# A's key weights by whole rows in one tile, with ScalarE's second weight load held back by a one-column copy

## The chip, the cores and the metric

The kernel runs on one core of one Trainium2 chip. The metric is device time in microseconds (us), the median over several executions. The hardware profiler records every instruction with its start and every DMA packet. The profiled span (470.8 us before) is about 2 us shorter than the device time of the same execution (472.58 us); the two are not mixed below.

The change can move well under 1 us of 473. A device time does not settle that: unaltered executions of the kernel before in one set of rounds ran from 472.62 to 473.16 us. So most of this study reads one mark in the profile: **the start of the 256th and last key matmul**. TensorE works without a pause from there to the end.

## The reference, cut to what matters

```python
def reference(A_x, A_wqkv, A_wo, B_x, B_wqkv, B_wo, gate_w):
    x = A_x                                    # 1 x 2048 x 1024, bf16
    g = sigmoid((x * gate_w).sum(-1))          # one gate per token
    a = linear_attention_A(x, A_wqkv, A_wo)    # 32 heads; phi(k) = where(k > 0, k + 1, exp(k)) + 1e-6
    b = sliding_attention_B(x, B_wqkv, B_wo)   # window 8, dilation 2
    return g * a + (1 - g) * b
```

The change touches only the first stage of A: the keys, `x @ A_wqkv[:, 1024:2048]`, then phi. In TensorE's terms, 16 token tiles (t) times 2 column halves times 8 contraction rows (kt, 128 each) give 256 matmuls of 128x512.

## The kernel before

The first loads. SyncE (`nc.sync`) and ScalarE (`nc.scalar`) each issue DMAs; `dma_start_transpose` delivers x with the contraction dimension on the partitions.

```python
    WkA = [wpool.tile([P, KT, 512], BF16, name=f"WkA{h}", tag="wa") for h in range(2)]

    def load_xT(k, t0, t1):        # two contraction rows, tokens of tiles t0..t1
        nc.sync.dma_start_transpose(out=xT[:, 2 * k:2 * k + 2, t0 * P:t1 * P],
                                    in_=rows(x, t0 * P, t1 * P)[:, 2 * k * P:(2 * k + 2) * P])

    def load_wk(eng, k, h):        # two contraction rows of one column half: 256 KB in runs of 1 KB
        eng.dma_start(out=WkA[h][:, 2 * k:2 * k + 2, :], in_=A_wqkv[..., D + 512 * h:D + 512 * h + 512] ...)

    with tc.manual_schedule(engines={SP, mybir.EngineType.Activation}):
        load_wk(nc.scalar, 0, 0)
        first_act = consts.tile([P, 1], BF16, name="first_act")
        nc.scalar.activation(out=first_act[:], in_=ones[:, 0:1], func=ACT.Exp)
        load_wk(nc.scalar, 0, 1)
        load_xT(0, 0, 2)
        load_xT(0, 2, 4)
        for k in range(1, 4):
            load_wk(nc.sync, k, 0)
            load_xT(k, 0, 4)
            load_wk(nc.sync, k, 1)
        ...                        # x for the other twelve token tiles, x by rows, later weights
```

The first matmuls, on eight PSUM banks, so that four token tiles and both halves advance together as the rows arrive:

```python
            warm_up(37)            # 37 matmuls of 128x128 on a constant
            first = [bank_k(i) for i in range(8)]
            for k in range(4):
                for half in range(2):
                    for t in range(4):
                        for kt in (2 * k, 2 * k + 1):
                            project(first[4 * half + t], t, kt, half)
                        if k == 3:
                            phi(work, pk[:, t, half * 512:(half + 1) * 512], first[4 * half + t])
            ...                    # token tiles 4 to 15, eight matmuls per bank
```

The softmax here doesn't subtract the row's maximum and nothing guards it: scores larger than these inputs give would overflow.

Of the kernel before, what the change touches and what calls it, by code (L numbers as in the profile page):

```python
# [8 lines left out]
ACT = mybir.ActivationFunctionType  # L9
ALU = mybir.AluOpType  # L10
BF16 = mybir.dt.bfloat16
# [4 lines left out]
P = 128  # L16
# [23 lines left out]
def kernel(  # L40
# [11 lines left out]
    nc = tc.nc  # L52
    S, D = A_x.shape[1:]
    assert D == 1024 and S == 2048

    x = A_x[0].rearrange("(m two) d -> two m d", two=2)
    out2 = out[0].rearrange("(m two) d -> two m d", two=2)

    def rows(ap, s0, s1):
        return ap[s0 // 1024, s0 % 1024:(s1 - 1) % 1024 + 1, :]  # L60
# [3 lines left out]
    KT = D // P  # L64
# [4 lines left out]

    consts = ctx.enter_context(tc.tile_pool(name="consts", bufs=1))  # L70
    wpool = ctx.enter_context(tc.tile_pool(name="wpool", bufs=2))
    dram = ctx.enter_context(tc.tile_pool(name="dram", bufs=1, space=bass.MemoryType.DRAM))
    big = ctx.enter_context(tc.tile_pool(name="big", bufs=1))
    ps_pj = ctx.enter_context(tc.tile_pool(name="ps_pj", bufs=4, space=bass.MemoryType.PSUM))

    def load_w(name, src, col0, tag, only=(0, 1)):
        halves = []
        for h in only:
            w = wpool.tile([P, KT, 512], BF16, name=f"{name}{h}", tag=tag)
            c0 = col0 + h * 512  # L80
            nc.sync.dma_start(out=w[:], in_=src[:, c0:c0 + 512].rearrange("(kt p) n -> p kt n", p=P))  # L81
            halves.append(w)
        return halves

    xT = big.tile([P, KT, S], BF16, name="xT", tag="xT")
    xrow = big.tile([P, NB, D], BF16, name="xrow", tag="vV")

    def load_rows(eng, t0, t1):
        eng.dma_start(out=xrow[:, t0:t1, :], in_=rows(x, t0 * P, t1 * P).rearrange("(t p) d -> p t d", p=P))  # L89

    WkA = [wpool.tile([P, KT, 512], BF16, name=f"WkA{h}", tag="wa") for h in range(2)]

    def load_xT(k, t0, t1):
        nc.sync.dma_start_transpose(out=xT[:, 2 * k:2 * k + 2, t0 * P:t1 * P],  # L94
                                    in_=rows(x, t0 * P, t1 * P)[:, 2 * k * P:(2 * k + 2) * P])

    def load_wk(eng, k, h):
        eng.dma_start(out=WkA[h][:, 2 * k:2 * k + 2, :],  # L98
                      in_=A_wqkv[2 * k * P:(2 * k + 2) * P, D + 512 * h:D + 512 * h + 512]
                      .rearrange("(kt p) n -> p kt n", p=P))  # L100

    ones = nc.const_aps.tensor(1.0, [P, P], BF16)
    with tc.manual_schedule(engines={SP, mybir.EngineType.Activation}):
        load_wk(nc.scalar, 0, 0)
        first_act = consts.tile([P, 1], BF16, name="first_act")
        nc.scalar.activation(out=first_act[:], in_=ones[:, 0:1], func=ACT.Exp)
        load_wk(nc.scalar, 0, 1)
        load_xT(0, 0, 2)
        load_xT(0, 2, 4)
        for k in range(1, 4):  # L110
            load_wk(nc.sync, k, 0)
            load_xT(k, 0, 4)
            load_wk(nc.sync, k, 1)
        for t in range(4, NB):
            nc.sync.dma_start_transpose(out=xT[:, :, t * P:(t + 1) * P], in_=rows(x, t * P, (t + 1) * P))  # L115
        for t in range(0, NB, 4):
            load_rows(nc.sync, t, t + 4)
        gw_row = consts.tile([P, D], BF16, name="gw_row")
        nc.sync.dma_start(out=gw_row[:], in_=gate_w.partition_broadcast(P))  # L119
        WvA = load_w("WvA", A_wqkv, 2 * D, "wb")  # L120
        WoA = load_w("WoA", A_wo, 0, "wo")
        WvB = load_w("WvB", B_wqkv, 2 * D, "wc")
    WqA = load_w("WqA", A_wqkv, 0, "wa")



# [13 lines left out]
    for slot in range(2):  # L140
        nc.gpsimd.memset(qsel[:, slot:slot + 1], 0.0)
        for pair in range(2):
            r = 64 * pair + 32 * slot
# [9 lines left out]
    def phi(work, dst, pj):  # L153
        e = work.tile([P, 512], F32, name="e", tag="e")
        nc.scalar.activation(out=e[:], in_=pj[:], func=ACT.Exp)  # L155
        nc.vector.tensor_scalar(out=e[:], in0=e[:], scalar1=1.0, scalar2=1e-6, op0=ALU.min, op1=ALU.add)  # L156
        nc.vector.scalar_tensor_tensor(out=dst, in0=pj[:], scalar=0.0, in1=e[:], op0=ALU.max, op1=ALU.add)

    with tc.manual_schedule(engines={PE}):

        with ExitStack() as s1:
# [4 lines left out]
            s1.enter_context(tc.manual_schedule(engines={DVE}))  # L166
            pk = big.tile([P, NB, D], BF16, name="pk", tag="pkO")
            def project(pj, t, kt, half):
                nc.tensor.matmul(pj[:], lhsT=xT[:, kt, t * P:(t + 1) * P], rhs=WkA[half][:, kt, :],  # L169
                                 start=(kt == 0), stop=(kt == KT - 1))  # L170

            def warm_up(n):
# [7 lines left out]
            def bank_k(i):  # L180
                return (ps_1.tile([P, 512], F32, name="pk1_ps", tag="p1") if i & 4 else
                        ps_pj.tile([P, 512], F32, name="pk_ps", tag="pj"))

            first = [bank_k(i) for i in range(8)]
            for k in range(4):
                for half in range(2):
                    for t in range(4):
                        for kt in (2 * k, 2 * k + 1):
                            project(first[4 * half + t], t, kt, half)
                        if k == 3:  # L190
                            phi(work, pk[:, t, half * 512:(half + 1) * 512], first[4 * half + t])
            for t in range(4, NB):
                for half in range(2):
                    pj = bank_k(2 * t + half)
                    for kt in range(KT):
                        project(pj, t, kt, half)
                    phi(work, pk[:, t, half * 512:(half + 1) * 512], pj)
# [6 lines left out]
            for t in range(1, NB):  # L204
                side.append(lambda t=t: nc.vector.tensor_tensor(
                    out=zacc[:], in0=zacc[:] if t > 1 else pk[:, 0, :], in1=pk[:, t, :], op=ALU.add))
            side.append(lambda: nc.gpsimd.partition_all_reduce(zrow[:], zacc[:], P, bass_isa.ReduceOp.add))
            for t in range(NB):
                side.append(lambda t=t: nc.vector.tensor_tensor_reduce(
                    out=gjunk[:], in0=xrow[:, t, :], in1=gw_row[:], scale=1.0, scalar=0.0, op0=ALU.mult,  # L210
# [3 lines left out]
            for half in range(2):  # L214
                g_ = junk.tile([P, KT, 512], BF16, name=f"G{half}", tag=f"G{half}")
                G.append(g_)
                for kt in range(KT):
                    pj = ps_pj.tile([P, 512], F32, name="g_ps", tag="pj")
                    for t in range(NB):
                        nc.tensor.matmul(pj[:], lhsT=xrow[:, t, kt * P:(kt + 1) * P],  # L220
                                         rhs=pk[:, t, half * 512:(half + 1) * 512],
# [12 lines left out]
            for g in range(2):  # L234
                kvp = ps_pj.tile([P, 512], F32, name="kv_ps", tag="pj")[:, 0:256].rearrange("p (c d) -> p c d", c=4)
                for c in range(4):
                    for kt in range(KT):
                        for j in range(2):
                            cols = slice(c * P + 64 * j, c * P + 64 * j + 64)
                            nc.tensor.matmul(kvp[64 * j:64 * j + 64, c, :], lhsT=WvA[g][:, kt, cols],  # L240
                                             rhs=G[g][:, kt, cols], start=(kt == 0), stop=(kt == KT - 1))
# [84 lines left out]
            def qa_units(t, bank, evacuate):  # L326
                def mm(half, kt, st):
                    if kt == 0:
                        st["pj"] = bank()
                    nc.tensor.matmul(st["pj"][:], lhsT=xT[:, kt, t * P:(t + 1) * P], rhs=WqA[half][:, kt, :],  # L330
                                     start=(kt == 0), stop=(kt == KT - 1))
                    if kt == KT - 1:
                        evacuate(t, half, st["pj"])
                for half in range(2):
                    st = {}
                    for kt in range(KT):
                        yield lambda half=half, kt=kt, st=st: mm(half, kt, st)
# [24 lines left out]
        with ExitStack() as s2:  # L362
# [163 lines left out]
            for c in range(KT):  # L526
                kts[c] = kpool.tile([P, 2, 1024], BF16, name="kt", tag="kt")
                for hh in range(2):
# [3 lines left out]
                    if 1 <= c <= 2:  # L532
                        t = 2 * (c - 1) + hh
                        nc.sync.dma_start_transpose(out=pqT[0][:, :, t * P:(t + 1) * P],
                                                    in_=pqd[t * P:(t + 1) * P, :])
                    if 4 <= c < 7:
# [6 lines left out]
                              in_=B_wo[4 * P:, 512:1024].rearrange("(k p) n -> p k n", p=P))  # L543
            raw = wpool.tile([P, 4, D], BF16, name="raw", tag="wc")
            fw = wpool.tile([P, 2, D], F32, name="fw", tag="wc")
            lw = wpool.tile([P, 4, D], BF16, name="lw", tag="wa")

            def qa_output(t, half):
                def lhsT(r, kt, j):
                    return xT[64 * r:64 * r + 64, kt, t * P + 64 * j:t * P + 64 * j + 64]  # L550

                def rhs(r, kt):
                    return WqA[half][64 * r:64 * r + 64, kt, :]

                def evacuate(ps, part):
                    if part == 0:
                        nc.scalar.copy(out=raw[:, t - 12, half * 512:(half + 1) * 512], in_=ps[:])
                return lhsT, rhs, evacuate
# [5 lines left out]
        with ExitStack() as s3:  # L564
# [54 lines left out]
            for i, p_ in enumerate(parts):  # L619
# [4 lines left out]
                f = out_part(i, *p_)  # L624
# [33 lines left out]
```

## Time and profile before

| | before |
|---|---|
| device time, median of 6 | 472.86 us (472.62 to 473.16) |
| profiled span | 470.8 us |
| TensorE busy | 465.1 us (99%) |
| last warm-up matmul starts | 4.63 us |
| first x piece has landed | 5.43 us |
| first / last key matmul starts | 5.48 / 60.52 us |

A semaphore is the counter that a DMA raises as its parts arrive and that an engine waits for; "landed" is the last of the sixteen semaphore records of a DMA. Those records, and starts to the hundredth, are read from the trace itself.

The first lines of the page of the kernel before. Section 1 gives each engine's busy time; of section 2 two rows are shown, where each digit is the busy tenths of one of 40 slices.

```profile
## 1 busy us (share of the span) xinstructions
PE 465.1 (99%) x5735; PEld 249.2 (53%) x5765; DVE 277.2 (59%) x600; ACT 169.7 (36%) x274; POOL 15.3 (3%) x30
## 2 busy tenths in 40 slices
PE   8999999999999999999999999999999999999997
...
DMA  8999970000644243527327525432563913211001
```

TensorE has no room except in the first slice and at the very end. The first slice, as the timeline shows it: columns are start in us, length in us, engine, line, operation, count, and in brackets how long the engine had been idle and what ended that. SPq and ACTq are the DMA issues of SyncE and ScalarE.

```profile
0.80 2.61 SPq L94 DMA_TRANSPOSE xT<-in_A_x_dram  x2
...
0.82 0.97 ACTq L98 DMA_DIRECT2D WkA<-in_A_wqkv_dram  x2
0.83 4.11 PE L175 MATMUL warm<-const-bfloat16-1.0 128*128 128x128 bf16 x37 [0.83 <-PEq L642]
...
2.09 0.20 ACT L106 ACTIVATE first_act<-const-bfloat16-1.0 128x1 bf16<-128x1 bf16 x1
3.46 0.58 SPq L98 DMA_DIRECT2D WkA<-in_A_wqkv_dram  x1
4.09 1.24 SPq L94 DMA_TRANSPOSE xT<-in_A_x_dram  x1
...
5.47 7.73 PE L169 MATMUL pk_ps<-WkA,xT 128*128 128x512 bf16 x34 [0.53 <-DMA xT<-in_A_x_dram]
```

Two things are to be seen. The key matmuls wait 0.53 us for x (0.73 us after the array could have taken the next matmul, 4.74), and then never again. And both of ScalarE's loads are issued at once, from 0.82 to 1.79: the Activation written between them holds nothing back, because it runs at 2.09, when the second load is already gone. (The idle time in brackets counts from the end of the matmul before, which the profile models. The other waits in the text count from start to start, less the usual pace, and so come out about 0.2 us longer.)

The same stretch by microseconds, with the DMA rate in the last column (columns: stretch, its length, TensorE's busy time and matmuls, granted clock, mean busy share of the DMA engines, GB/s):

```profile
core 0: us, PE busy (x), PEclk, DMA share, GB/s
2.50:3.50 1.00, 1.00 (x12) 1.00 1.09 309
3.50:4.50 1.00, 1.00 (x12) 1.00 1.13 327
4.50:5.50 1.00, 0.47 (x6) 1.00 1.00 227
5.50:6.50 1.00, 1.00 (x5) 1.00 1.11 251
```

### The profile page before, as it was taken

The page shows a single profiled execution, that of the slowest core. Times are in us where ns is not written, and L with a number is a line of the kernel's source. Part 1 is how long each engine was busy: PE and PEld are TensorE (multiplying, and loading weights), DVE is VectorE, ACT ScalarE, POOL GpSimd, SP SyncE. Part 2 cuts the span into 40 slices and gives each one's busy share as a digit, 9 for nine tenths or more (in the row PEclk, how much of TensorE's full clock was granted, in tenths as well). Part 3 has the DMA queues.
Part 4 walks back from the last instruction along what each step waited for, and adds up shares of the span by engine and source line. Part 5 has one row for each costly group of instructions (what it writes and reads, how often), then busy time and mean ns, then how long its engine had stood idle before and what let it go on. Part 6 is the DMA issues. An engine that isn't in the chain of part 4 may idle for free.

```text
span 470.8 us, 13145 instructions
## 1 busy us (share of the span) xinstructions
PE 465.1 (99%) x5735; PEld 249.2 (53%) x5765; DVE 277.2 (59%) x600; ACT 169.7 (36%) x274; POOL 15.3 (3%) x30
## 2 busy tenths in 40 slices
PE   8999999999999999999999999999999999999997
PEld 5444444445444444444677677777764444444444
DVE  0586689990319999999567676767670049800000
ACT  1343321112533333334555555555551134221121
POOL 2300000500000000000000000000000000000000
PEclk9999999999999999999999999999999999999999
DMA  8999970000644243527327525432563913211001
GB/s 208 207 237 377 349 254 0 0 1 1 208 141 123 79 143 125 155 97 250 104 55 111 109 48 94 101 88 57 92 167 73 232 59 79 71 53 46 34 33 46
DMA packets 98732, 55.40 MB, mean 118 GB/s; under 512 B 70130, under 2 KB 90610, under 8 KB 98674
## 3 DMA queue, kind: packets, MB, share of 16 engines
q1 hardware_dynamic: 93378, 49.87, 40.6%
q10 hardware_dynamic: 5296, 4.69, 2.9%
q8 instruction: 45, 0.74, 0.7%
q14 instruction: 13, 0.11, 0.1%
HBM read 26.10 MB, written 15.86 MB: 89 GB/s over the span
## 4 chain that ended last, share of the span: by engine, by line
PE 85%; SPq 11%; DMA 2%; DVE 1%; issue 1%; ACT 0%; DVEq 0%
PE q_ps L389 27%; PE d_ps L593 12%; PE e_ps L593 11%; PE g_ps L220 11%; PE p_ps L294 11%; PE p_ps L330 8%; SPq L115 4%; SPq L81 4%; DMA WvB<-in_B_wqkv_dram 2%; PE po L468 2%; PE s2b L446 2%; SPq L94 1%; SPq L119 1%; SPq L98 1%; SPq L89 1%
## 5 line engine op out<-in xcount | busy, mean ns | idle before, releaser
L389 PE MATMUL q_ps<-xT,WqB 64*64 64x512 bf16 x1024 | 69.0, 377 | 0.0
L389 PE MATMUL q_ps<-xT,WkB 64*64 64x512 bf16 x1024 | 68.5, 376 | 0.0
L156 DVE TENSOR_SCALAR e<-e 128x512 f32<-128x512 f32 x64 | 27.1, 423 | 65.9 <-ACT e L155 65.9
L294 PE MATMUL p_ps<-WvB,xT 128*128 128x512 bf16 x250 | 57.3, 379 | 0.4
L169 PE MATMUL pk_ps<-WkA,xT 128*128 128x512 bf16 x251 | 55.2, 379 | 0.8 <-DMA xT<-in_A_x_dram 0.5
L220 PE MATMUL g_ps<-pk,xrow 128*128 128x512 bf16 x251 | 55.2, 379 | 0.3
L451 ACT ACTIVATE PT<-s2b 128x928 bf16<-128x928 f32 (+4 forms) x40 | 34.1, 854 | 45.2 <-PE s2b L446 45.2
L453 DVE TENSOR_TENSOR PT<-PT,mask 128x928 bf16<-128x928 bf16 (+4 forms) x40 | 23.6, 590 | 35.9 <-ACT PT L451 35.9
L330 PE MATMUL p_ps<-WqA,xT 128*128 128x512 bf16 x188 | 43.0, 379 | 0.2
L593 PEld LDWEIGHTS <-pqT 128*128 128x128 bf16 x272 | 26.0, 98 | 29.7 <-issue 0.4
L593 PEld LDWEIGHTS <-OBT 128*128 128x128 bf16 x272 | 26.0, 98 | 29.4
L169 PEld LDWEIGHTS <-xT 128*128 128x128 bf16 x256 | 25.0, 98 | 30.8 <-DMA xT<-in_A_x_dram 0.8
L220 PEld LDWEIGHTS <-xrow 128*128 128x128 bf16 x256 | 25.0, 98 | 30.2
L294 PEld LDWEIGHTS <-xT 128*128 128x128 bf16 x256 | 24.8, 98 | 30.2 <-issue 0.7
L389 PEld LDWEIGHTS <-WkB 64*64 64x64 bf16 x1024 | 32.6, 107 | 12.4 <-DMA vd<-tmp 0.2
L389 PEld LDWEIGHTS <-WqB 64*64 64x64 bf16 x1024 | 31.6, 107 | 11.1 <-issue 0.2
L600 DVE TENSOR_SCALAR osb<-e_ps,omg 128x128 bf16<-128x128 f32 x1 | 0.3, 350 | 57.6 <-PE e_ps L593 57.6
L155 ACT ACTIVATE e<-pk_ps 128x512 f32<-128x512 f32 x32 | 18.9, 597 | 40.4 <-PE pk_ps L169 36.1
L299 ACT CAST tmp<-p_ps 128x512 bf16<-128x512 f32 x32 | 18.7, 588 | 36.4 <-PE p_ps L294 32.5
L593 PE MATMUL d_ps<-WoA,pqT 128*128 128x512 bf16 (+1 forms) x133 | 30.7, 369 | 0.2
L593 PE MATMUL d_ps<-WoB,OBT 128*128 128x512 bf16 (+1 forms) x134 | 30.7, 369 | 0.1
L330 PEld LDWEIGHTS <-xT 128*128 128x128 bf16 x192 | 18.8, 98 | 22.7
(63 smaller groups left out, 528.5 us busy)
## 6 DMA issues: line engine op xcount, KB each, us to landing
vd<-tmp SPq DMA_DIRECT2D x16, 264.0 KB
xrow<-in_A_x_dram SPq DMA_DIRECT2D x4, 1024.0 KB
out_dram<-osb ACTq DMA_DIRECT2D x31, 128.0 KB
pqd<-tmp SPq DMA_DIRECT2D x12, 256.0 KB
WvA<-in_A_wqkv_dram SPq DMA_DIRECT2D x2, 1024.0 KB
WoA<-in_A_wo_dram SPq DMA_DIRECT2D x2, 1024.0 KB
WvB<-in_B_wqkv_dram SPq DMA_DIRECT2D x2, 1024.0 KB
WqA<-in_A_wqkv_dram SPq DMA_DIRECT2D x2, 1024.0 KB
```

Of the source, the lines that this page charges most:

```text
L81: nc.sync.dma_start(out=w[:], in_=src[:, c0:c0 + 512].rearrange("(kt p) n -> p kt n", p=P))
L115: nc.sync.dma_start_transpose(out=xT[:, :, t * P:(t + 1) * P], in_=rows(x, t * P, (t + 1) * P))
L155: nc.scalar.activation(out=e[:], in_=pj[:], func=ACT.Exp)
L156: nc.vector.tensor_scalar(out=e[:], in0=e[:], scalar1=1.0, scalar2=1e-6, op0=ALU.min, op1=ALU.add)
L169: nc.tensor.matmul(pj[:], lhsT=xT[:, kt, t * P:(t + 1) * P], rhs=WkA[half][:, kt, :], start=(kt == 0), stop=(kt == KT - 1))
L220: nc.tensor.matmul(pj[:], lhsT=xrow[:, t, kt * P:(kt + 1) * P], rhs=pk[:, t, half * 512:(half + 1) * 512], start=(t == 0), stop=(t == NB - 1))
L294: nc.tensor.matmul(st["pj"][:], lhsT=xT[:, kt, t * P:(t + 1) * P], rhs=WvB[half][:, kt, :], start=(kt == 0), stop=(kt == KT - 1))
L330: nc.tensor.matmul(st["pj"][:], lhsT=xT[:, kt, t * P:(t + 1) * P], rhs=WqA[half][:, kt, :], start=(kt == 0), stop=(kt == KT - 1))
L389: nc.tensor.matmul(banks[o][64 * j:64 * j + 64, :], lhsT=lhsT(r, kt, j), rhs=rhs(r, kt), start=first and kt == 0, stop=kt == KT - 1, skip_ ...
L451: nc.scalar.activation(out=pt[:, :, 0:W_], in_=s2b[:].rearrange("p a b s -> p (a b) s")[:, :, 0:W_], func=ACT.Exp, scale=SCALE)
L453: nc.vector.tensor_tensor(out=pt[:, :, 0:W_], in0=pt[:, :, 0:W_], in1=mask[:, None, base:base + W_].broadcast_to([P, 4, W_]), op=ALU.mult)
L593: nc.tensor.matmul(st["ps"][:, 0:n], lhsT=lhsT, rhs=W[c0 // 512][:, c, c0 % 512:c0 % 512 + n], start=(side == 0 and c == 0), stop=(side == ...
```

## The change

The intent: one tile of whole rows instead of two of column halves, so that each weight run is 2 KB and the first step needs just row 0 of the weights and row 0 of x; the second load of ScalarE (now row 2) is really held back, by a copy that writes one column of its destination, so that x row 0 does not share the queues with it; the rest of the weights is threaded between x pieces of one or two rows. The order of the first 64 matmuls follows. `WqA`, which reuses the space, becomes one tile too.

```diff
@@ -88,29 +89,29 @@
     def load_rows(eng, t0, t1):
         eng.dma_start(out=xrow[:, t0:t1, :], in_=rows(x, t0 * P, t1 * P).rearrange("(t p) d -> p t d", p=P))
 
-    WkA = [wpool.tile([P, KT, 512], BF16, name=f"WkA{h}", tag="wa") for h in range(2)]
-
-    def load_xT(k, t0, t1):
-        nc.sync.dma_start_transpose(out=xT[:, 2 * k:2 * k + 2, t0 * P:t1 * P],
-                                    in_=rows(x, t0 * P, t1 * P)[:, 2 * k * P:(2 * k + 2) * P])
-
-    def load_wk(eng, k, h):
-        eng.dma_start(out=WkA[h][:, 2 * k:2 * k + 2, :],
-                      in_=A_wqkv[2 * k * P:(2 * k + 2) * P, D + 512 * h:D + 512 * h + 512]
-                      .rearrange("(kt p) n -> p kt n", p=P))
+    WkA = wide.tile([P, KT, D], BF16, name="WkA", tag="wa")
+
+    def load_xT(kt, n, t0, t1):
+        nc.sync.dma_start_transpose(out=xT[:, kt:kt + n, t0 * P:t1 * P],
+                                    in_=rows(x, t0 * P, t1 * P)[:, kt * P:(kt + n) * P])
+
+    def load_wk(eng, kt):
+        eng.dma_start(out=WkA[:, kt, :], in_=A_wqkv[kt * P:(kt + 1) * P, D:2 * D])
 
     ones = nc.const_aps.tensor(1.0, [P, P], BF16)
     with tc.manual_schedule(engines={SP, mybir.EngineType.Activation}):
-        load_wk(nc.scalar, 0, 0)
-        first_act = consts.tile([P, 1], BF16, name="first_act")
-        nc.scalar.activation(out=first_act[:], in_=ones[:, 0:1], func=ACT.Exp)
-        load_wk(nc.scalar, 0, 1)
-        load_xT(0, 0, 2)
-        load_xT(0, 2, 4)
-        for k in range(1, 4):
-            load_wk(nc.sync, k, 0)
-            load_xT(k, 0, 4)
-            load_wk(nc.sync, k, 1)
+        load_wk(nc.scalar, 0)
+        nc.scalar.copy(out=WkA[:, 2, 0:1], in_=ones[:, 0:1])
+        load_wk(nc.scalar, 2)
+        load_xT(0, 1, 0, 4)
+        load_wk(nc.sync, 1)
+        load_xT(1, 1, 0, 4)
+        load_xT(2, 2, 0, 4)
+        load_wk(nc.sync, 3)
+        for kt in (4, 6):
+            load_wk(nc.sync, kt)
+            load_xT(kt, 2, 0, 4)
+            load_wk(nc.sync, kt + 1)
         for t in range(4, NB):
             nc.sync.dma_start_transpose(out=xT[:, :, t * P:(t + 1) * P], in_=rows(x, t * P, (t + 1) * P))
         for t in range(0, NB, 4):
@@ -120,7 +121,10 @@
         WvA = load_w("WvA", A_wqkv, 2 * D, "wb")
         WoA = load_w("WoA", A_wo, 0, "wo")
         WvB = load_w("WvB", B_wqkv, 2 * D, "wc")
-    WqA = load_w("WqA", A_wqkv, 0, "wa")
+    WqA = wide.tile([P, KT, D], BF16, name="WqA", tag="wa")
+    for h in range(2):
+        nc.sync.dma_start(out=WqA[:, 4 * h:4 * h + 4, :],
+                          in_=A_wqkv[512 * h:512 * h + 512, 0:D].rearrange("(kt p) n -> p kt n", p=P))
 
 
 
@@ -182,12 +186,12 @@
                         ps_pj.tile([P, 512], F32, name="pk_ps", tag="pj"))
 
             first = [bank_k(i) for i in range(8)]
-            for k in range(4):
+            for kts_ in ((0,), (1,), (2, 3), (4, 5), (6, 7)):
                 for half in range(2):
                     for t in range(4):
-                        for kt in (2 * k, 2 * k + 1):
+                        for kt in kts_:
                             project(first[4 * half + t], t, kt, half)
-                        if k == 3:
+                        if kts_[-1] == KT - 1:
                             phi(work, pk[:, t, half * 512:(half + 1) * 512], first[4 * half + t])
             for t in range(4, NB):
                 for half in range(2):
... (the same indexing change where WqA and the tile lw are used; a new pool for the wide tile)
```

More of the change, by code (lines that the diff above doesn't have):

```diff
@@ L71 @@
     wpool = ctx.enter_context(tc.tile_pool(name="wpool", bufs=2))
+    wide = ctx.enter_context(tc.tile_pool(name="wide", bufs=1))
     dram = ctx.enter_context(tc.tile_pool(name="dram", bufs=1, space=bass.MemoryType.DRAM))
@@ L168, in project @@
             def project(pj, t, kt, half):
-                nc.tensor.matmul(pj[:], lhsT=xT[:, kt, t * P:(t + 1) * P], rhs=WkA[half][:, kt, :],
+                nc.tensor.matmul(pj[:], lhsT=xT[:, kt, t * P:(t + 1) * P], rhs=WkA[:, kt, half * 512:half * 512 + 512],
                                  start=(kt == 0), stop=(kt == KT - 1))
@@ L329, in mm @@
                         st["pj"] = bank()
-                    nc.tensor.matmul(st["pj"][:], lhsT=xT[:, kt, t * P:(t + 1) * P], rhs=WqA[half][:, kt, :],
+                    nc.tensor.matmul(st["pj"][:], lhsT=xT[:, kt, t * P:(t + 1) * P], rhs=WqA[:, kt, half * 512:half * 512 + 512],
                                      start=(kt == 0), stop=(kt == KT - 1))
@@ L545 @@
             fw = wpool.tile([P, 2, D], F32, name="fw", tag="wc")
-            lw = wpool.tile([P, 4, D], BF16, name="lw", tag="wa")
+            lw = wide.tile([P, 4, D], BF16, name="lw", tag="wa")
             def qa_output(t, half):
@@ L552, in rhs @@
                 def rhs(r, kt):
-                    return WqA[half][64 * r:64 * r + 64, kt, :]
+                    return WqA[64 * r:64 * r + 64, kt, half * 512:half * 512 + 512]
                 def evacuate(ps, part):
```

## The prediction

> **What bounds it now.** TensorE. The page's busy table gives PE 465.1 us of 470.8 (99%); the granted clock is full throughout. By the trace's start times the 128x512 key matmuls run 0.2158 us start to start, the figure of the Trainium skill, "TensorE: Matmul & The Clock Gate", for a warm array (N / 2.4 GHz + about 2.5 ns). After the first key matmul no gap exceeds 0.45 us, and the 0.43 us ones recur every 10.8 us, as lost records would. The only real idle stretch is at the start: the last warm-up matmul starts at 4.63 (pitch 0.107), so the array is free at 4.74; the first key matmul starts at 5.47, just after the first x piece's semaphore at 5.43 (waits view: "DMA xT<-in_A_x_dram"). That is 0.73 us, and all the change can win; the rest follows rigidly.
>
> **Why x is late.** DMA packets by queue: the first x piece's data move from 2.85 to 3.8 us, but its semaphore packets appear at 4.2 to 4.4, only after ScalarE's second weight load (issued 1.34) has moved its 256 KB from 3.4 to 4.3. The Activation meant to stand between the two loads holds nothing back: it runs at 2.09.
>
> **What changes.**
> - The copy writes a column of row 2's destination, so that load really waits: issue about 2.35 instead of 1.34. Then only row 0 stands beside the first x piece (also 128 KB), which should land at about 4.6 (4.4 to 5.0) instead of 5.43. First key matmul at 4.75 to 5.0.
> - Rows of 2 KB instead of 1 KB: later 1 MB loads show 2.7 us with 2 KB rows (xrow) and 3.0 us with 1 KB rows (WvA), so each 256 KB is about 0.07 us cheaper, 0.6 us over eight. The Trainium skill, "DMA: Bandwidth & Descriptors", "Why small descriptors are slow", agrees in kind.
> - DMA issues: two on ScalarE, eleven on SyncE, as before; transposes about 1.25 us each.
> - Same matmuls, other order: row 0, row 1, then pairs. But a step now needs whole rows. With a first matmul at 4.75, row 1 is needed at 6.5, x rows 2 and 3 at 8.2, weight row 3 at 8.4, row 5 at 11.9. Loads in those places of the queue landed before at 7.7 (x), 8.3 to 9.5 (weights) and 12.5. Less the cheaper rows: about 7.5, 8.5 to 9.2, and 12.1. So the earlier start is bought with slack: before, every load after the first few came at least 1.1 us early. I expect 0.1 to 0.8 us of new stalls, at row 3 and perhaps row 5 or x row 1.
> - WqA loads after the last key matmul (60.5 instead of 59.2), lands before 70, used after 130: free. lw waits for the same late matmuls: free.
>
> **On the critical path.** Start -0.6, stalls +0.3: net -0.3 us, shifting the end rigidly.
>
> **Predicted time:** 472.6 us; 8 in 10 between 472.0 and 473.2. Faster by over 2%: 0.5%; within 2%: 99%; slower by over 2%: 0.5%.
>
> **What would show it.** First x landing below 5 us and first key matmul near 4.8. Row 2's issue after the copy, near 2.35. Gaps among the first 64 key matmuls naming WkA or xT loads, summing to 0.1 to 0.8 us; the last key matmul near 60.2 (60.5 before). Nothing else changed.
>
> **What would make it wrong.** If x's landing does not depend on the second weight load, the start stays at 5.4. If rows 3 or 5 straggle, stalls eat more than the start gives: 0.5 us slower. If rows come well early, the whole 0.7 us is won.

## The result, and the profile after

| | before | after |
|---|---|---|
| device time, median of 6 | 472.86 us (472.62 to 473.16) | 472.89 us (472.71 to 473.31) |
| profiled span | 470.8 us | 471.1 us |
| first x piece has landed | 5.43 us | 4.11 us |
| first key matmul starts | 5.48 us | 4.37 us |
| wait inside the first 64 key matmuls | none | 1.35 us, before the ninth |
| last key matmul starts | 60.52 us | 60.77 us |

The ratio of the times is 1.0001 with a 95% interval of 0.9988 to 1.0014: the same time. (A ratio is the mean time of one kernel's fast runs over that of the other's fast runs of the same rounds, so it is not quite the ratio of the medians quoted.) The interval is 0.6 us wide on either side, about as much as the start could have won (0.73).

The timeline of the changed kernel, to be held against the one above:

```profile
0.80 1.24 SPq L95 DMA_TRANSPOSE xT<-in_A_x_dram  x1
...
0.83 0.39 ACTq L99 DMA_DIRECT2D WkA<-in_A_wqkv_dram  x1
0.84 3.69 PE L179 MATMUL warm<-const-bfloat16-1.0 128*128 128x128 bf16 x37 [0.84 <-PEq L646]
...
2.10 0.19 ACT L104 COPY WkA<-const-bfloat16-1.0 128x1 bf16<-128x1 bf16 x1
2.10 0.56 SPq L99 DMA_DIRECT2D WkA<-in_A_wqkv_dram  x1
2.32 0.34 ACTq L99 DMA_DIRECT2D WkA<-in_A_wqkv_dram  x1
2.71 2.48 SPq L95 DMA_TRANSPOSE xT<-in_A_x_dram  x2
...
4.37 1.89 PE L173 MATMUL pk_ps<-WkA,xT 128*128 128x512 bf16 x8
...
7.45 5.79 PE L173 MATMUL pk_ps<-WkA,xT 128*128 128x512 bf16 x26 [1.19 <-DMA xT<-in_A_x_dram]
```

The holding back works: the copy ends at 2.29 and row 2's load is issued at 2.32 instead of 1.34. The first key matmul follows the warm-up without a gap. But after eight matmuls, all that row 0 allows, TensorE waits for x row 1, which lands at 7.40. The chain of waits of the changed kernel now begins there (start in us, length, what):

```profile
2.71 4.70 DMA xT<-in_A_x_dram
7.45 53.70 PE pk_ps L173 x248
61.15 55.25 PE g_ps L224 x256
```

And the stretches by microseconds:

```profile
core 0: us, PE busy (x), PEclk, DMA share, GB/s
2.50:3.50 1.00, 1.00 (x12) 1.00 1.03 290
3.50:4.50 1.00, 1.00 (x15) 1.00 0.86 48
4.50:5.50 1.00, 1.00 (x7) 1.00 0.97 326
5.50:6.50 1.00, 0.76 (x4) 1.00 1.37 271
6.50:7.50 1.00, 0.05 (x1) 1.00 1.16 218
```

Between 3.5 and 4.5 us the queues moved 48 GB/s where before they moved 327. The busy share of the DMA engines is 0.86 all the same, so it hides this: fifteen 2 KB packets of row 1, starting between 3.55 and 4.05, are recorded as taking 0.63 to 1.15 us each, against 0.084 for most others (the expectations below say sixteen; one of the sixteen was quick). The difference, 327 - 48 = 279 GB/s over one microsecond, is about 280 KB, a little more than one whole weight row (256 KB). So a first account suggests itself: what the early start won, the loads behind it lost. The experiments test both halves of it.

### The profile page after: what moved, and what is told of

It reads as the page before. It is cut to its first block, busy times and chain, and to the rows that moved or that the text cites. A ratio compares the mean times of both kernels' runs of the same rounds, so it can differ in the third digit from the quotient of the medians.

```text
span 471.1 us, 13175 instructions
## 1 busy us (share of the span) xinstructions
PE 466.3 (99%) x5765; PEld 248.9 (53%) x5765; DVE 277.2 (59%) x600; ACT 169.8 (36%) x274; POOL 15.4 (3%) x30
## 4 chain that ended last, share of the span: by engine, by line
PE 98%; DMA 1%; SPq 0%; DVE 0%; issue 0%; DVEq 0%
PE q_ps L393 27%; PE d_ps L597 12%; PE p_ps L298 12%; PE g_ps L224 12%; PE e_ps L597 12%; PE pk_ps L173 11%; PE p_ps L334 9%; PE po L472 2%; PE s2b L450 2%; DMA xT<-in_A_x_dram 1%; PE kv_ps L244 0%; PE w_ps L287 0%; SPq L95 0%; SPq L99 0%; DVE osb L604 0%
```

## The experiments

Twelve more runs were made: eight new kernels, and second profiles of four. All gave correct results. `after_again`, `no_hold`, `hold_old`, `hold_long` and `swap_single_x_again` ran on one chip, `before_again`, `hold_old_long`, `swap` and `row2_sp` on a second, the other three on a third, so comparisons across these groups also compare chips. In each profile the last key matmul is at "first key matmul + 55.03 us of matmuls + waits".

### The two kernels again

`before_again` and `after_again` are the two kernels unaltered, for a second profile each.

> The kernel before, unaltered, for a second profile: first x piece at 5.2 to 5.7, first key matmul right after it, no other stall over 0.1 us, last key matmul at 60.3 to 60.8. It shows how far two profiles of one kernel differ in these marks.

> The changed kernel, unaltered, for a second profile. If the slow second weight load of the first profile (row 1: sixteen packets of 0.63 to 1.15 us each from 3.55 us on, landing 6.81) and the 1.35 us stall of TensorE behind x row 1 belong to the order of the loads, both come back: x row 0 lands near 4.1, x row 1 near 7.4, stall 1.2 to 1.5 us. If the slow packets were an accident of one run, row 1 lands near 5.5, x row 1 near 6.5 and the stall is under 0.6 us.

| profile | x first lands | x row 1 lands | first key matmul | waits or slow pace | last key matmul |
|---|---|---|---|---|---|
| before | 5.43 | (with row 0) | 5.48 | 0.0 | 60.52 |
| before_again | 5.12 | (with row 0) | 5.17 | 0.0 | 60.22 |
| after | 4.11 | 7.40 | 4.37 | 1.37 | 60.77 |
| after_again | 4.18 | 7.35 | 4.60 | 1.08 | 60.71 |

The wait before the ninth matmul repeats (1.35 and 1.07 us; the later start of `after_again` makes its wait shorter) and so does the landing of x row 1. `before_again` landed its first x piece at 5.12, just outside the expected 5.2 to 5.7. Single profiles of one kernel differ by up to 0.3 us in the mark, which bounds what can be read from one. In times, `after_again` ran in 472.79 us and `before_again` in 472.26 us, beside the kernel before at 472.82 (seven runs) and 472.36 (one run).

### The change without the holding back: `no_hold`

```diff
-        nc.scalar.copy(out=WkA[:, 2, 0:1], in_=ones[:, 0:1])
+        first_act = consts.tile([P, 1], BF16, name="first_act")
+        nc.scalar.copy(out=first_act[:], in_=ones[:, 0:1])
         load_wk(nc.scalar, 2)
```

> Row 2 no longer held back: the copy writes a tile of its own, so ScalarE issues row 2 near 1.34 us. Theory A (the second load on ScalarE's queue delays the first x piece): x row 0 lands at 5.0 to 5.5 instead of 4.1 and the first key matmul comes there; row 2 is then through before row 1 and x row 1, so x row 1 lands no later than with the hold (7.0 to 7.4) and the stall after the first eight matmuls shrinks to 0.2 to 0.6 us; the last key matmul comes within 0.3 us of the changed kernel's. Rival B (the smaller shape of the x piece, one row by 512 tokens, brought it early): x row 0 still lands by 4.3.

Measured: row 2 is issued at 1.28; x row 0 lands at 5.04 and the first key matmul starts at 5.09. Theory A holds and rival B falls: with whole rows and the one-row x piece in place, x is still late as long as ScalarE's second load is issued early. x row 1 lands at 6.88 (a little earlier than expected), the waits after the start are 0.10 us at x row 1 (0.2 to 0.6 was expected) and 0.24 at row 3, and the last key matmul starts at 60.48, 0.2 to 0.3 us *before* the changed kernel's. That difference is no larger than the one between two profiles of one kernel; in these profiles the earlier start of the changed kernel is not worth anything at the mark. The device time of the one run was 473.17 us; in that execution TensorE lost 0.6 us near 351 us, among the late A queries, where this edit changes nothing.

The key matmuls of `no_hold`, to be held against the two lines of the changed kernel:

```profile
5.09 9.15 PE L174 MATMUL pk_ps<-WkA,xT 128*128 128x512 bf16 x40 [0.26 <-DMA xT<-in_A_x_dram]
```

The stretches of `no_hold`:

```profile
core 0: us, PE busy (x), PEclk, DMA share, GB/s
2.50:3.50 1.00, 1.00 (x12) 1.00 1.08 273
3.50:4.50 1.00, 1.00 (x12) 1.00 1.15 323
4.50:5.50 1.00, 0.74 (x7) 1.00 1.23 245
```

One edit, the holding back, takes the stretch from 3.5 to 4.5 us from 323 to 48 GB/s (92 in `after_again`, which ran on the same chip as `no_hold`). This is the main evidence for the second half of the account: ScalarE's second load, issued early, is what fills that microsecond. By queues, 0.24 of the 0.32 MB that `no_hold` moved in it were ScalarE's; in the changed kernel ScalarE's queue moved 0.01 MB.

### The holding back alone, on the kernel before: `hold_old`

```diff
-        first_act = consts.tile([P, 1], BF16, name="first_act")
-        nc.scalar.activation(out=first_act[:], in_=ones[:, 0:1], func=ACT.Exp)
+        nc.scalar.activation(out=WkA[1][:, 0, 0:1], in_=ones[:, 0:1], func=ACT.Exp)
         load_wk(nc.scalar, 0, 1)
```

> The kernel before with the holding back alone: the first Activation writes a column of the second weight load's destination; rows, halves, pieces and order are those of before. Theory A: the first x piece lands near 4.1 to 4.4 instead of 5.43, the first key matmul starts when the warm-up ends (4.4 to 4.8), and since the second x piece and the second weight half then come late, a stall appears at the third or the ninth matmul, 0.3 to 1.0 us; net 0 to 0.6 us earlier at the last key matmul (60.52 before). Rival B: first x piece still at 5.2 or later, nothing moves.

Measured: the first x piece lands at 4.82 instead of 5.43 and 5.12 (its first part at 4.10), the first key matmul starts at 4.87. That is later than theory A's 4.1 to 4.4 and earlier than rival B's 5.2, so it leans to theory A; the pair before is the cleaner proof. But the second x piece lands at 7.98 instead of 5.65 and the waits and a slow pace at the start sum to 2.31 us, 2.03 of it one wait before the fifth matmul, far over the 0.3 to 1.0 expected.

```profile
4.87 1.29 PE L168 MATMUL pk_ps<-WkA,xT 128*128 128x512 bf16 x4
8.03 6.22 PE L168 MATMUL pk_ps<-WkA,xT 128*128 128x512 bf16 x28 [1.87 <-DMA xT<-in_A_x_dram]
```

The last key matmul starts at 62.21 and the time is 474.09 us against 472.82 of the kernel before (ratio 1.0016, interval 0.9995 to 1.0037: one run of the kernel before took 474.45 in these rounds, so the times alone do not resolve it). By the mark of its one profile, then, the holding back taken alone is a loss of 1.7 to 2.0 us.

### Holding back longer: `hold_long` and `hold_old_long`

In both, the instruction that holds the load back writes 1024 columns instead of one, so the load is issued at 3.17.

```diff
 # hold_long, on the changed kernel
-        nc.scalar.copy(out=WkA[:, 2, 0:1], in_=ones[:, 0:1])
+        nc.scalar.copy(out=WkA[:, 2, :].rearrange("p (a b) -> p a b", b=P),
+                       in_=ones[:, None, :].broadcast_to([P, 8, P]))
 # hold_old_long, on the kernel before
-        nc.scalar.activation(out=first_act[:], in_=ones[:, 0:1], func=ACT.Exp)
+        nc.scalar.activation(out=WkA[1][:, 0:2, :].rearrange("p k (a b) -> p (k a) b", b=P),
+                             in_=ones[:, None, :].broadcast_to([P, 8, P]), func=ACT.Exp)
```

> The changed kernel with row 2 held back about 1 us longer: the copy writes the whole row, 1024 columns. Theory C (x row 1 is late because row 2's 256 KB run beside row 1's, ahead of it): row 1 lands near 6.0 instead of 6.8 and x row 1 at 6.5 to 6.9 instead of 7.4, the stall before the ninth matmul falls to 0.5 to 0.9 us, with perhaps a new one at row 2. Rival D (row 1's sixteen first packets are slow by themselves, just after the x transpose): they stay at 0.6 to 1.1 us, row 1 lands no earlier than 6.3 and the stall stays over 1 us.

> The kernel before with its second weight half held back about 1 us longer than in the run that held it back by one column (1024 columns written: issue near 3.2 us). If the second x piece was late there because the half was issued in the middle of its own issue and went ahead of it, it lands at 5.0 to 5.8 here instead of 7.98, the half at 6.0 to 7.0, the first key matmul starts at 4.4 to 4.8 and the stalls sum to 0 to 0.8 us: last key matmul 59.8 to 60.6. If holding back always costs about 2 us of stall in this layout, the last key matmul stays near 62.2.

`hold_long` went against theory C's numbers: x row 1 lands at 8.38, later instead of earlier, and the wait grows to 2.07 us (last key matmul 61.74). Row 1 did land earlier (6.22), but row 2's load was now issued at 3.17, in the middle of x row 1's own issue (2.72 to 3.91), and ran beside it. Rival D got slow first packets right (nine of row 1's took over 0.6 us) and the landing of row 1 nearly (6.22 against "no earlier than 6.3"), but it does not explain why x row 1 moved by a microsecond.

`hold_old_long` did as expected: the second x piece lands at 5.33, the second weight half at 7.08 (a little late), the wait for it is 0.74 us, the last key matmul starts at 60.46. So the same hold, a microsecond longer, costs 1.75 us less in one layout (62.21 to 60.46) and a microsecond more in the other. That fits the held load being harmful by what it meets when it is let go; but each of these is one profile, and the two on the kernel before ran on different chips.

### Other loads in that place: `swap` and `row2_sp`

```diff
 # swap: rows 1 and 2 exchange queues
         load_wk(nc.scalar, 0)
-        nc.scalar.copy(out=WkA[:, 2, 0:1], in_=ones[:, 0:1])
-        load_wk(nc.scalar, 2)
+        nc.scalar.copy(out=WkA[:, 1, 0:1], in_=ones[:, 0:1])
+        load_wk(nc.scalar, 1)
         load_xT(0, 1, 0, 4)
-        load_wk(nc.sync, 1)
         load_xT(1, 1, 0, 4)
+        load_wk(nc.sync, 2)
         load_xT(2, 2, 0, 4)
 # row2_sp: no second load on ScalarE; the copy goes to a tile of its own
-        load_wk(nc.scalar, 2)
         load_xT(0, 1, 0, 4)
         load_wk(nc.sync, 1)
         load_xT(1, 1, 0, 4)
+        load_wk(nc.sync, 2)
```

> The changed kernel with rows 1 and 2 changing queues: ScalarE issues row 0 and, held back by the same one-column copy, row 1; SyncE issues x row 0, x row 1, then row 2, x rows 2 and 3 and the rest. Theory E (an x piece issued while a weight load is on the other queue, or behind whole weight rows, waits for their bytes; before x row 1 stood 512 KB of rows 1 and 2, here only row 1's 256 KB): x row 0 near 4.1, x row 1 at 5.3 to 6.2 instead of 7.4, stall before the ninth matmul 0 to 0.2 us; the next weak place is x rows 2 and 3 and row 3 (needed at start + 3.5 and + 3.7), stall there 0.3 to 1.0; last key matmul 60.0 to 60.5 (changed kernel 60.7 to 60.8). Rival F (any second load in this phase costs about a microsecond of idle queues, whoever waits for it): row 1 lands at 6.5 or later and the stall before the ninth matmul stays near 1 us.

> The changed kernel with no second load on ScalarE's queue: row 2 goes on SyncE's queue behind x row 1. Theory E: x row 0 near 4.1, x row 1 now behind row 1 alone, at 5.6 to 6.5; stall before the ninth matmul 0 to 0.4; in exchange row 2 adds a SyncE issue of about 0.6 us, so x rows 2 and 3 land at 8.4 to 9.2 and the stall moves to the step of rows 2 and 3: in all 0.6 to 1.4 us, last key matmul 60.0 to 60.9. Rival D (row 1's first packets are slow by themselves behind the x transpose): sixteen packets of 0.6 to 1.1 us between 3.5 and 4.8 again, with nothing on the other queue, and x row 1 at 6.3 or later.

Theory E holds: with only one weight row about it, x row 1 lands at 6.48 (`swap`) and 6.08 (`row2_sp`) instead of 7.40. Rival F fell by its numbers: row 1 landed at 5.99 in `swap`, not at 6.5 or later (the nearly idle queues that it speaks of are there all the same, 119 GB/s from 3.5 to 4.5 us). Rival D fell too: in `row2_sp` only one of row 1's packets exceeded 0.55 us, and x row 1 landed well before 6.3. In neither was there a wait for x row 1.

The last key matmul still came only at 60.57 and 60.97. In both, something happened that none of the expectations had: the first four (`swap`) and five (`row2_sp`) key matmuls ran wholly or partly at half pace. The trace shows it in starts and lengths, here the first six key matmuls of `swap` (an ordinary listing: start in us, length in ns):

```
4.735 634
5.162 634
5.588 634
6.015 547
6.398 380
6.615 379
```

The Trainium skill, "TensorE: Matmul & The Clock Gate", section "Wait — 56ns, not 53.3ns?", gives 426.7 ns start to start for a cold array at N = 512 and 215.7 for a warm one; the trace has 427 and 216. So the array's clock had not come up when x was already there. The page's column of granted clock does not show it; it says 1.00 in that stretch of `swap`:

```profile
4.70:5.70 1.00, 0.96 (x3) 0.00 (x0) 0.00 (x0) 1.00 1.10 231
```

(Here the columns after TensorE are VectorE and ScalarE; the granted clock is the third number from the end.) The slow pace is only part of why the mark did not move. In `row2_sp` TensorE then waited 0.27 us for row 3, needed by the eighteenth matmul and landed at 9.56; from there on the mark is fixed, whatever the pace before. In `swap` row 3 landed at 8.93: an estimate, 8.93 plus 238 starts 0.2158 us apart, gives a mark no earlier than 60.3 at full pace, so the slow pace cost at most about 0.3 us.

### Is the slow start an accident: `swap_again`

> The kernel with rows 1 and 2 on exchanged queues, unaltered, for a second profile. In its first profile x row 1 landed at 6.48 instead of 7.4 and no wait was left at it, but the first four key matmuls ran 0.43 us apart, twice the usual, as in the run with row 2 on SyncE's queue; all others of this study started at 0.216. Theory G (the array's clock had not come up yet at 4.74 in those two executions, and when it comes up varies from run to run; the warm-up's own pitch tells): where the warm-up's last matmuls are 0.06 apart the key matmuls start at 0.216 and the last key matmul comes at 60.0 to 60.4 with a wait of 0.1 to 0.7 us left at x row 1 or row 3; where they are 0.107 apart the first ones are slow again and it stays near 60.5. Rival H (the slow pace belongs to this order of loads): slow first matmuls also behind a 0.06 warm-up.

The warm-up of this execution ended at the fast pace and the key matmuls began at 0.216 us: theory G holds and rival H falls. All profiles fit G: the first matmul always starts at 0.84 us, and the last one at the full slow pace starts between 3.5 us (`hold_old_long`) and 6.0 us (`row2_sp`). (The expectation's "all others" overlooks `hold_old`, a different order of loads, whose first key matmuls also ran 398 and 293 ns apart, behind a warm-up that was slow to its end.)

But the last key matmul came at 61.60, not at 60.0 to 60.4: row 3, which had landed at 8.93 in the first profile of the same kernel, landed at 10.19 in this one, and TensorE waited 1.63 us for it.

```profile
10.23 4.04 PE L173 MATMUL pk_ps<-WkA,xT 128*128 128x512 bf16 x18 [1.45 <-DMA WkA<-in_A_wqkv_dram]
```

Such slow spells occur in the profiles of the kernel before as well. There the second half of the second weight pair landed at 9.52 in both profiles, its first part at 8.26. It was needed only at 10.65, so it cost nothing.

### A version that might beat both: `swap_single`, `swap_single_x`, `swap_single_x_again`

To `swap`, two steps were added: TensorE takes rows 2 and 3 one by one, so that row 3 is needed 1.5 us later (`swap_single`), and row 2's weights also go behind x rows 2 and 3 on SyncE's queue (`swap_single_x`, run twice).

```diff
-            for kts_ in ((0,), (1,), (2, 3), (4, 5), (6, 7)):
+            for kts_ in ((0,), (1,), (2,), (3,), (4, 5), (6, 7)):
 # swap_single_x, besides
-        load_wk(nc.sync, 2)
         load_xT(2, 2, 0, 4)
+        load_wk(nc.sync, 2)
```

> Exchanged queues, and TensorE takes rows 2 and 3 one by one instead of as a pair, so that row 3's weights are needed 1.5 us later. By the landings of the exchanged run (x row 1 6.48, row 2 7.24, x rows 2 and 3 8.29, row 3 8.93) the start that needs no wait falls from 5.26 to about 4.85 us. If the early loads alone decide, the last key matmul comes at 59.8 to 60.3 (60.2 and 60.5 for the kernel before, 60.7 and 60.8 for the changed kernel) and the time is 0.2 to 0.6 us below before's: ratio 0.9987 to 0.9996, hardly resolved. If the clock is late in an execution, 60.3 to 60.6 and no gain.

> As the run before it, with row 2's weights behind x rows 2 and 3 on SyncE's queue. x rows 2 and 3 should land near 7.6 instead of 8.3, row 2 near 8.2, row 3 unchanged near 8.9: start without a wait at about 4.7 to 4.8. Last key matmul 59.7 to 60.3 with the clock up, ratio of times 0.9985 to 0.9996.

> The best candidate once more, unaltered, for a second interval and a second profile. Its first ratio was 0.9987 with an interval of 0.9971 to 1.0004. If it gains what its landings promise (0.2 to 0.6 us of 473), the ratio comes between 0.9985 and 0.9998 again; if the first ratio was luck, it comes within 0.0005 of 1. In the profile: last key matmul 59.7 to 60.4 unless one of the early loads is held up by a slow spell of the queues, as row 3 was in the second profile of the exchanged kernel (landing 10.19 instead of 8.93), in which case it is 61 or later.

| run | median | before | ratio (95% interval) | last key matmul |
|---|---|---|---|---|
| swap_single | 472.74 us | 472.82 us | 1.0002 (0.9983 to 1.0021) | 60.85 |
| swap_single_x | 472.59 us | 472.82 us | 0.9987 (0.9971 to 1.0004) | 60.31 |
| swap_single_x_again | 472.37 us | 472.74 us | 0.9992 (0.9978 to 1.0006) | 60.34 |

`swap_single` met its own bad luck: x row 1 at 7.12, a wait of 0.60 there and 0.37 later. `swap_single_x` is the better one: both medians lie 0.2 to 0.4 us below the kernel before (the first ratio is flattered by one execution of the kernel before at 474.86 us; without it the mean of the other ten is 0.3 us above that of `swap_single_x`, where the ratio says 0.6) and both profiles have the last key matmul at 60.3, although the array was cold for the first one to three key matmuls in both. (Both profiled executions also paused later, for 0.6 and 0.1 us.) Each interval still contains 1, so no version is shown to be faster. Its landings also show what a margin is worth: row 3 landed at 9.59 and 9.95, late like the 10.19 that cost `swap_again` a wait, and here no wait came of it because row 3 is needed later. The second of the two did wait 0.31 us for row 5.

## Why the prediction was right or wrong

The time was inside the range (472.89 in 472.0 to 473.2) and in the predicted class. The small gain forecast, 0.3 us, is not seen: the device times differ by 0.03 us with 0.6 us of uncertainty, and the mark in the profiles went the other way, from 60.52 and 60.22 to 60.77 and 60.71, where 60.2 had been forecast. That the time fell inside the range says little for the account: the range is wider than all that the change could win (0.73 us), and an early start and long waits, both larger than forecast, nearly cancelled.

- **What bounds the kernel: right.** All the change could win was the wait before the first key matmul; everything after the last key matmul is rigid (407.32 to 407.34 us).
- **Why x was late: right, and shown.** Holding back ScalarE's second load brings the first x piece from 5.04 (`no_hold`) to 4.11 and 4.18, with nothing else changed; on the kernel before, from 5.43 and 5.12 to 4.82. The Trainium skill, "DMA: Bandwidth & Descriptors", section "Queues, rings and completion order", offers a reason: a DMA's semaphore write lands only after every earlier write of that DMA engine, across its queues. The trace agrees in time (x's semaphore packets at 4.2 to 4.4, as the other load ends at 4.3), but no run separates this from descriptors being generated in order of issue.
- **The holding back: right.** Issue at 2.32, forecast near 2.35.
- **The start: right in kind, under-sized.** Forecast 4.75 to 5.0; it was 4.37 and 4.60. x landed at 4.11 and 4.18 (forecast 4.4 to 5.0), and the warm-up ended sooner in these executions because the array's clock came up during it.
- **The 2 KB rows: right in kind, and small.** Two loads issued back to back (rows 3 and 4) land 0.68 and 0.66 us apart in the two profiles of the changed kernel; the corresponding loads of the kernel before, in 1 KB runs, 0.73 and 0.71. The next such pair has 0.69 and 0.68 against 0.71 and 0.73. Forecast: 0.07 us per load.
- **"I expect 0.1 to 0.8 us of new stalls, at row 3 and perhaps row 5 or x row 1": this is the step that failed, in its size and its place.** The waits were 1.37 and 1.08 us, and all at x row 1. Row 3 did land where forecast (9.16 and 8.92, for 8.5 to 9.2), and so did row 5 (12.01; 11.13 in the second profile), but with TensorE already delayed neither was waited for. Row 3 stood close behind, though: by the estimate used for `swap`, its landings alone would have kept the mark at 60.5 and 60.3 or later, so curing x row 1 would not have won the forecast 0.3 us for certain.
- **Why that term was mis-sized.** The forecast gives no landing time for x row 1. A mark of 60.2 needs it by about 6.9 (60.2 less 247 starts 0.2158 us apart); it came at 7.40 and 7.35, and at 6.88 in `no_hold`. So the half microsecond by which the mark missed the forecast matches what the hold added to x row 1 in these profiles. The rest of the wait is no loss at the mark: it grows by as much as the start comes early. The forecast let the loads behind x row 0 flow on at the old rate. They do not. From 3.5 to 4.5 us the queues moved 327 and 331 GB/s in the two profiles of the kernel before and 323 in `no_hold`, the three with ScalarE's second load issued by 1.34; in the eleven others, where that load is held back or absent, 48 to 192. Row 1 was issued at 2.10 and row 2 at 2.32, and neither comes at its full rate before about 4.5. So the hold leaves the queues nearly empty for most of a microsecond, and then both rows, 512 KB, go ahead of x row 1. The empty microsecond alone does not make x row 1 late: `swap` and `row2_sp` had it too (119 and 192 GB/s) and landed x row 1 at 6.48 and 6.08, with only one weight row about it. The pair that differs by the hold alone is `no_hold` and the changed kernel.
- **WqA and lw: right.** WqA landed at 69.1 (70.0 before) and is first used after 130; the unchanged time from the mark to the end shows no cost of either.

What is left of x row 1's lateness goes with its neighbourhood. How long an x piece takes from its own issue to its landing varies with the weight loads issued about it (the pieces differ in shape, and only `no_hold` against the changed kernel, `hold_long` against it, and `hold_old` against `hold_old_long` are pairs that differ in the time of one load's issue alone):

| x piece | weight load about it | issue to landing, us |
|---|---|---|
| row 0, `after`, `after_again`, `row2_sp` | only row 0, issued with it | 3.3, 3.4, 3.3 |
| first piece, `hold_old`, `hold_old_long` | only the first half, issued with it | 4.0, 3.8 (first part 3.3 in both) |
| row 1, `row2_sp` | row 1 just before it, same queue | 3.4 |
| second piece, `before`, `hold_old_long` | second half over before it; second half issued at the end of its issue | 3.5, 3.2 |
| first piece, `before`, `before_again`; row 0, `no_hold` | a second load issued in the middle of its issue | 4.6, 4.3, 4.2 |
| row 1, `swap`, `swap_again`, `swap_single` (4.4 in both of `swap_single_x`) | row 1 issued in the middle of its issue | 4.4, 4.4, 5.0 |
| row 1, `after`, `after_again` | rows 1 and 2 both just before it | 4.7, 4.6 |
| second piece, `hold_old`; row 1, `hold_long` | a held load issued in the middle of its issue | 5.8, 5.7 |

What stays open: whether the half microsecond that the hold added to x row 1 would repeat in a second profile of `no_hold`; why a load that is issued at 2.1 us streams only from about 4.5 when nothing is waiting in front of it, and why whole-queue slow spells of half a microsecond to a microsecond fall where they do. No run separates descriptor generation from memory here. Also open is whether `swap_single_x` is faster: two intervals, 0.9971 to 1.0004 and 0.9978 to 1.0006, lean that way and do not settle it.

## What to carry to other kernels

Holding one load back to let another land first was not free here: look at the DMA rate in the microsecond after the favoured load, and at what stands before the next piece, because if nothing has been issued to fill the gap, the gain at the front can come back as a wait at the next piece. When finer steps let a kernel start earlier, count how much earlier than its use each later load lands: the kernel before started about 0.7 us late but had about 1.1 us or more in hand at the loads behind its first x pieces, and so was untouched by slow spells that cost the earlier starters 0.3 to 1.6 us. Below a few tenths of a microsecond, use a fixed mark in several profiles and not one of them; the landing of the same load in the same kernel moved by up to 1.3 us.

## What the Trainium skill lacked or had wrong

- "DMA: Bandwidth & Descriptors", section "Issuing engines are not separate DMA queues", says that issuing from several engines saves only the sequencer's time. It does not say what the moment of issue does to the DMAs of the other engine. Here the issue time of a load on the other queue decided when an x piece landed: row 2 issued at 1.28 or 2.32 us gave x row 0 at 5.04 or 4.11, and the rate from 3.5 to 4.5 us at 323 or 48 GB/s. The page has no word on a transposing load taking longer when a plain load is issued in the middle of its issue (3.2 to 3.5 us against 4.2 to 5.8, in most of the cases of the table above).
- The same page gives a first-byte latency for these queues of about 0.6 us, in "Latency and other measured facts". In the changed kernel row 1, issued from 2.10 to 2.66, had its first packet at 3.41 and its full rate at about 4.5. Counted from the end of the issue, the first packet took 0.75 us, near the page's figure; the page does not say from where it counts, and lacks the time to full rate behind another load.
- No page that was consulted mentions spells in which a dozen to two dozen packets, about one for each DMA engine, are held for 0.4 to 1.9 us and mostly let go within some hundredths of a microsecond. They are in all profiles here, for instance 16.3 to 18.0 us in the changed kernel; the same load of one kernel landed at 8.93 and at 10.19.
- "TensorE: Matmul & The Clock Gate", section "What's actually happening", says that the moment of warming up varies by about half a microsecond (its note on 6, 11 or 14 cold matmuls in one kernel allows more), and its table in "Why this matters for your kernels" advises at least 4 us of matmuls first. Here the last matmul at the full slow pace started 2.6 to 5.2 us after the first one, over fourteen profiles, and in three of them over 4 us after it, so 4 us would not always have been enough. The same page's statement that the activity window runs free of the kernel fits there being a spread; no run here shows the window itself.
- The granted-clock column of the profile says 1.00 while matmuls run 427 ns apart. "TensorE: Matmul & The Clock Gate", section "Seeing it yourself", warns that the clock events of a trace have been seen to be unreliable on trn2, but does not name this case. Start-to-start times show the cold array (427 against 216 ns), and so does the length of one (634 against 379 ns).
